# A second pair of bf16 q/k buffers, state transfers a chunk later, and a written order for the transfer queue, in a kernel of chunked mLSTM attention and a bilinear MLP

## Chip, cores and metric

One core of a Trainium2 chip runs the kernel. The metric is device time in microseconds; several runs are taken, and their median counts. Five engines work side by side: PE (matmul), DVE (vector), ACT (scalar), POOL (GpSimd) and SP, which here does nothing but issue DMA transfers.

## The reference

The first part is an mLSTM recurrence over 768 tokens for 4 batches of 8 heads of width 40; the second is a bilinear MLP on the 3072 tokens of 320 channels.

```python
for t in range(S):
    m_new = np.maximum(f_gate[:, :, t] + m, i_gate[:, :, t])
    f_stab = np.exp(f_gate[:, :, t] + m - m_new)
    i_stab = np.exp(i_gate[:, :, t] - m_new)
    C = f_stab * C + i_stab * einsum('bhd,bhe->bhde', vt, kt)
    n = f_stab * n + i_stab * kt
    denom = np.maximum(np.abs(n . qt), 1.0)
    y[:, :, t] = sigmoid(o_gate[:, :, t]) * (C qt) / denom
x = y.transpose(0, 2, 1, 3).reshape(B * S, H * D)
out = ((x @ w_a) * (x @ w_b)) @ w_out
```

(The indices that broadcast are left out.) All inputs and the output are float32.

## The kernel before

**Chunks and blocks.** The recurrence is computed chunk by chunk: 24 chunks `n`, six spans of 128 tokens for each of four batches, numbered so that a batch comes again after four chunks. A chunk needs its own q, k, v and gates and the state that the same batch's last chunk left. The MLP works on nine blocks of two or three chunks (`sizes`). `run_block(kb)` puts the MLP of block `kb` and the attention of block `kb + 1` into one order on PE: after each MLP matmul it gives out as many steps of `attention()` as are due by a count (`units`), so that attention is done shortly before its block's MLP ends. From block 2 on, PE's order is exactly this written one; the other queues are ordered by a scheduler, by when it thinks things come due.

**A late chunk** (n from 6 on) is a set of generators, each a stage cut at its `yield`s, and the string `PATTERN` says whose next step comes. `stage_a(n+1)` splits q and k into three bf16 pieces: ACT casts the first (L432), DVE makes the others, all in a `qks` buffer, one for q and one for k, and SP transposes it to `T` (L446, two transfers a buffer; `T` too has one buffer for q and one for k). `stage_b` computes the scores `pS` from `T` (L469), weighs them by the gate table `E` (a tile `gbc`, L474) and casts them to `pb` (L476, L480). `stage_i` computes `pI` from q and the state `cx` (L495). `stage_c` computes `pV` from `pb`, `E` and v (L521), so it is the last reader of that `gbc` tile; there are two `gbc` buffers, and `load_g` (L180) fills one for chunk n + 2. `stage_u` updates the state `cst` (`pU`, L545), splits it into `cb`, sends that to `c_dram` and reads it back as `cx`, side by side as PE needs it (L573 to L577). `stage_e(n+1)` masks the gate table on POOL (L407) and takes its exponentials on ACT (L414). `stage_f` divides by the denominator and multiplies by the output gates `osig` (L597, L600, L602); `load_o` loads four chunks' gates at once and ACT takes their sigmoid (L167). `stage_d` transposes the result to `xh`, `xl` for the MLP (L620 to L626).

**The MLP of a block** runs over 12 groups `ff` of 128 hidden units. `up` makes two products `pu_ff_0` and `pu_ff_1` of eight matmuls each (L729; three PSUM buffers for all `pu`); ACT (DVE for two groups) copies the first to `g` (L736), DVE multiplies it with the second (L737) and splits it into `gh` and `gl` (L739, L741). `down`, two groups later, adds into `pd` (L702). After the last group ACT copies each `pd` to a tile `o` (L711) and SP stores it (L712). The tiles `g` and `o` have one tag, `acp`, with three buffers.

**The gates** of all chunks are computed once at the start, in scratch tiles `gfim`, `g_tab` and `g_b`; the conversion of the MLP's weights uses the two `qks` buffers as its scratch (`step`) before attention needs them.

Of the kernel before, what the change touches and what calls it, by code (L numbers as in the profile page):

```python
# [8 lines left out]
F32 = mybir.dt.float32  # L9
BF16 = mybir.dt.bfloat16  # L10
# [10 lines left out]
def kernel(  # L21
# [45 lines left out]
    for x in qk:  # L67
        nc.gpsimd.memset(x[..., D:], 0.0)
    va = [wpool.tile([P, H, DV], F32, name=f"va{j}") for j in range(NQ)]
    qks2 = [wpool.tile([P, 2, H, P], BF16, name=f"qks{j}") for j in range(2)]  # L70

    step = [
        x.rearrange("p w h t -> p (w h t)").bitcast(F32)[:, j * WCH:(j + 1) * WCH]
        for j in range(2) for x in qks2
    ]
    HH = H // 2

# [74 lines left out]
    def load(n):  # L152
        with tc.issue_after(issued.get(("v", n - 1), issued["w"])):
            load_qk(n)
            load_v(n)
# [28 lines left out]

        return x.bitcast(BF16).rearrange("p h (d w) -> p h d w", w=2)[:, :, :, 1]

    gfim = wpool.tile([3 * BH, S], F32, name="gfim")
    gf, gi, gm = (gfim[j * BH:(j + 1) * BH] for j in range(3))
    tab = wpool.tile([3 * BH, NC, P], F32, name="g_tab")
    gbt = wpool.tile([3 * BH, 2, P], F32, name="g_b")  # L190
    gb3 = [gbt[j * BH:(j + 1) * BH] for j in range(3)]

    def fetch_gates(cols):
        for t, x in ((gf, f_gate), (gi, i_gate)):
# [223 lines left out]
    def stage_a(n):  # L418

        c, b = chunks[n]  # L420
        s = st.setdefault(n, {})
        src = nat(n)[0][..., 0:D]
        need(32)
        for _ in conv:
            pass

        at = {"h": (0, 2 * D), "m": (D, D), "l": (2 * D, 0)}
        s["T"] = []
        for j in range(2):
            qks = qks2[j]  # L430
            ph, pm, pl = (qks[:, 1, :, at[i][j]:at[i][j] + D] for i in "hml")
            nc.scalar.copy(ph, src[:, j])  # L432
            yield
            r = apool.tile([P, H * DV], F32, tag="tmp", name=f"r{n}_{j}")[:, 0:H * D]
            r = r.rearrange("t (h d) -> t h d", h=H)
            (nc.gpsimd if 2 * n + j < 4 else nc.vector).tensor_tensor(r, src[:, j], ph, op=ALU.subtract)  # L436
            nc.vector.tensor_copy(pm, r)
            yield
            (nc.gpsimd if n < 8 else nc.vector).tensor_tensor(pl, r, pm, op=ALU.subtract)
            yield  # L440
            lo = (1 - j) * D
            nc.vector.tensor_copy(qks[:, 0, :, lo:lo + 2 * D], qks[:, 1, :, D - lo:3 * D - lo])
            nc.vector.tensor_copy(qks[:, 0, :, 2 * D * j:2 * D * j + D], ph)  # L443
            T = apool.tile([P, 2, H, P], BF16, tag=f"T{j}", name=f"T{n}_{j}", bufs=1)
            for w in range(2):
                nc.sync.dma_start_transpose(T[:, w], qks[:, w].rearrange("t h d -> t (h d)"))  # L446
            s["T"].append(T)
            yield
# [84 lines left out]
    def stage_u(n):  # L533
        c, b = chunks[n]
        if c == NC - 1:
            return
        s = st[n]
        if n < 6:
            pU = ps_dn.tile([P, 512], F32, tag="pd2", name=f"pU{n}")
        else:  # L540
            pU = ps_at.tile([P, 512], F32, tag="pat", name=f"pU{n}")
        pu = pU[:, 0:HH * DV].rearrange("p (h d) -> p h d", h=HH)
        for h in range(H):
            r, _, x = half(h)
            nc.tensor.matmul(  # L545
                pu[r:r + 64, x], nat(n)[0][:, 1, h, :], s["vw"][:, h], start=True, stop=True
            )
# [12 lines left out]
        cb = apool.tile([P, 3, HH, DV], BF16, tag="cb", name=f"cb{n}", bufs=1)  # L560
        cr = apool.tile([P, H * DV], F32, tag="tmp", name=f"cr{n}")[:, 0:HH * DV]
        cr = cr.rearrange("t (h d) -> t h d", h=HH)
        nc.scalar.copy(cb[:, 2], t)
        nc.gpsimd.tensor_tensor(cr, t, cb[:, 2], op=ALU.subtract)
        yield
        if n < 8:
            nc.scalar.copy(cb[:, 1], cr)
        else:
            nc.vector.tensor_copy(cb[:, 1], cr)
        nc.gpsimd.tensor_tensor(cb[:, 0], cr, cb[:, 1], op=ALU.subtract)  # L570
        for j in range(2):
            cd = c_dram[b][:, :, j * HH:(j + 1) * HH].rearrange("i d h e -> d i h e")
            nc.sync.dma_start(cd[:, 3], cb[j * 64:j * 64 + D, 2])  # L573
            nc.sync.dma_start(cd[:, 0:3], cb[j * 64:j * 64 + D])
        for w in range(2):
            nc.sync.dma_start(
                cx[b][w], c_dram[b][w:w + 3].rearrange("i d h e -> (i d) h e")  # L577
            )
        yield

    def stage_f(n):
        s = st[n]
        num = s["num"]
        nq = num[:, :, D]
        den = apool.tile([P, H], F32, tag="den", name=f"den{n}")
        if chunks[n][0] == 0:
            nc.vector.tensor_scalar(den, nq, -1.0, 1.0, op0=ALU.mult, op1=ALU.max)
            nc.vector.scalar_tensor_tensor(den, nq, 1.0, den, op0=ALU.mult, op1=ALU.max)
        else:
            nc.vector.scalar_tensor_tensor(den, nq, -1.0, nq, op0=ALU.mult, op1=ALU.max)  # L590
            nc.vector.tensor_scalar_max(den, den, 1.0)
        after["r", n] = nc.vector.reciprocal(den, den).ins  # L592
        yield
        c, b = chunks[n]
        y = osig[c][:, b]
        yv = y[:, 0:DM].rearrange("p (h d) -> p h d", h=H)
        (nc.vector if n < NS else nc.gpsimd).tensor_tensor(  # L597
            yv, yv, den.unsqueeze(2).broadcast_to([P, H, D]), op=ALU.mult
        )
        nc.vector.tensor_tensor(yv, num[:, :, 0:D], yv, op=ALU.mult)  # L600

        nc.scalar.copy(y[:, DM:], y[:, 2 * P:DM])  # L602
        s["y"] = y
        yield

# [23 lines left out]
        yield ("done", n)  # L629


    PATTERN = "bebebBeBeBeiaaadadadoaaavcvcfufuu"

    def ahead(n):
        if n + 1 < NCH:
            if n > NS:
                with tc.issue_after(issued["w"]):
                    load(n + 1)
        if NE <= n + 2 < NCH:
            load_g(n + 2)  # L640

    def gates_in(n):
        if n % B == 0 and n > 0:
            load_o(n // B)

    def early_chunk(n):
        yield from begin_b(n)
        yield from begin_i(n)
        if n > NS:
            yield from stage_d(n - 1)  # L650
        gates_in(n)
        yield from (begin_e if n + 1 < NE else stage_e)(n + 1)
        if n + 1 < NF32:
            yield from begin_a(n + 1)
        else:
            yield from stage_a(n + 1)
            yield from stage_v(n + 1)
        yield from begin_c(n)
        yield from stage_u(n)
        yield from stage_f(n)  # L660

    def late_chunk(n):
        more = n + 1 < NCH
# [314 lines left out]
    def rest():  # L978
# [75 lines left out]
```

## Time and profile before

| | us |
|---|---|
| runs: median (lowest to highest) | 583.01 (582.88 to 584.32) |
| the profiled execution | 583.91 |
| its span, first to last instruction | 582.1 |
| PE busy | 545.8 (94%) |
| DVE busy | 411.3 (71%) |
| ACT busy | 225.6 (39%) |
| POOL busy | 126.2 (22%) |

The profile shows one execution. Busy times overlap, and matmuls are pipelined, so 94% is no measure of PE's pace: that is told by the granted clock, 0.950 in the mean of the span. Views of the trace name an instruction by engine, line and tiles, and give the idle time of its engine just before it with what ended it; "SPq" is SP's issuing of transfers.

### The profile page before, as it was taken

What the parts mean: (1) busy time and instruction counts of PE and PEld (TensorE: products, weight loads), DVE (VectorE), ACT (ScalarE), POOL (GpSimd) and SP (SyncE); (2) the same over time, 40 slices, a digit from 0 to 9 for tenths busy, and PEclk for the clock granted to TensorE, in tenths of its full rate; (3) what the DMA queues carried; (4) which work ended last, traced back from release to release, by engine and by line L of the source; (5) the groups of instructions that cost most, each with busy time, mean ns of one, the idle gap of its engine ahead of it and who ended that gap; (6) DMA issues with size and microseconds to landing.
All of it is one profiled execution on the core that took longest, in us unless ns stands there. A gap on an engine that the chain in (4) does not pass through costs nothing.

```text
span 582.1 us, 12451 instructions
## 1 busy us (share of the span) xinstructions
PE 545.8 (94%) x4810; PEld 515.7 (89%) x4810; DVE 411.3 (71%) x949; ACT 225.6 (39%) x548; POOL 126.2 (22%) x181
## 2 busy tenths in 40 slices
PE   9687899998999997999799998999989999999997
PEld 6585799988998996999799997998989999999997
DVE  6899776469978883887749876778848675944332
ACT  5677745334432542332523432523313533311111
POOL 2011235253331230332221340331211202000000
PEclk9686679998999997999899999999989999999999
DMA  9999513577949745478555577486536532400000
GB/s 177 288 269 270 116 32 90 114 105 159 157 115 149 147 92 106 84 150 162 103 125 101 116 124 134 112 158 141 92 85 122 113 73 90 56 1 24 0 1 35
DMA packets 198679, 66.77 MB, mean 115 GB/s; under 512 B 184252, under 2 KB 191900, under 8 KB 198620
## 3 DMA queue, kind: packets, MB, share of 16 engines
q1 hardware_dynamic: 198620, 65.98, 55.1%
q8 instruction: 38, 0.62, 0.5%
q14 instruction: 21, 0.17, 0.1%
HBM read 41.11 MB, written 5.97 MB: 81 GB/s over the span
## 4 chain that ended last, share of the span: by engine, by line
PE 71%; issue 6%; DMA 4%; DVE 3%; SPq 2%; ACT 1%; POOL 1%; POOLq 0%; ACTq 0%; DVEq 0%
PE pu L729 40%; PE pd L702 18%; DMA T<-qks 4%; PE pV L521 3%; PE pS L469 2%; PE pU L545 2%; SPq L446 1%; PE pS L803 1%; PE pV L855 1%; PE pX L620 1%; PE pI L495 1%; PE pI L824 1%; DVE g L737 1%; PE pT L790 0%; POOL osig L597 0%
## 5 line engine op out<-in xcount | busy, mean ns | idle before, releaser
L729 PE MATMUL pu<-xh,w 128*128 128x384 f32 (+1 forms) x1080 | 289.5, 333 | 4.2 <-ACT g L736 1.8
L729 PE MATMUL pu<-xl,w 128*128 128x384 f32 (+1 forms) x648 | 211.8, 329 | 1.0 <-DVE xl L626 1.0
L729 PEld LDWEIGHTS pu<-xh,w 128*128 128x128 f32 x1080 | 196.6, 196 | 7.9 <-DVE w L374 3.0
L702 PE MATMUL pd<-w,gh 128*128 128x320 f32 x576 | 133.8, 319 | 8.8 <-DVE gh L739 8.0
L729 PEld LDWEIGHTS pu<-xl,w 128*128 128x128 f32 x648 | 126.9, 196 | 1.6 <-DVE xl L626 1.3
L702 PEld LDWEIGHTS pd<-w,gh 128*128 128x128 f32 x576 | 99.6, 194 | 10.2 <-DVE gh L739 8.9
L737 DVE TENSOR_TENSOR g<-pu,g 128x384 f32<-128x384 f32 (+1 forms) x108 | 54.7, 506 | 52.2 <-PE pu L729 49.0
L702 PE MATMUL pd<-w,gl 128*128 128x320 f32 x288 | 91.1, 322 | 0.1
L736 ACT COPY g<-pu 128x384 f32<-128x384 f32 (+1 forms) x92 | 40.4, 439 | 76.8 <-PE pu L729 69.5
L456 POOL TENSOR_TENSOR vr<-va 128x336 f32<-128x336 f32 x18 | 14.5, 804 | 203.0 <-PE pV L521 203.0
L702 PEld LDWEIGHTS pd<-w,gl 128*128 128x128 f32 x288 | 54.9, 193 | 0.9 <-DVE gl L741 0.6
L432 ACT CAST qks<-qk 128x320 bf16<-128x320 f32 x36 | 16.5, 458 | 96.2 <-DMA T<-qks 84.5
L414 ACT ACTIVATE gbc<-gbc,gtab 128x128 f32<-128x128 f32 x160 | 49.3, 389 | 9.9 <-POOL gbc L407 9.8
L741 DVE TENSOR_TENSOR gl<-g,gh 128x384 fp32r<-128x384 f32 (+1 forms) x92 | 48.3, 525 | 1.3
L443 DVE COPY qks<-qks 128x320 bf16<-128x320 bf16 x36 | 10.6, 296 | 42.4 <-ACT qks L432 37.6
L739 DVE CAST gh<-g 128x384 fp32r<-128x384 f32 (+1 forms) x96 | 36.4, 379 | 1.4
L476 ACT CAST pb<-gbc 128x512 bf16<-128x512 f32 x36 | 22.1, 613 | 27.3 <-DVE gbc L474 27.3
L436 DVE TENSOR_TENSOR r<-qk,qks 128x320 f32<-128x320 f32 x36 | 26.1, 725 | 2.1 <-ACT qks L432 2.1
L597 POOL TENSOR_TENSOR osig<-osig,den 128x320 f32<-128x320 f32 x22 | 15.9, 723 | 53.5 <-DVE den L592 43.6
L407 POOL TENSOR_SCALAR_AFFINE_SELECT gbc<-gbc 128x1024 f32<-128x1024 f32 x20 | 24.4, 1221 | 14.1 <-DMA gbc<-g_dram 13.5
L521 PEld LDWEIGHTS <-pb 128*128 128x128 bf16 x576 | 23.1, 96 | 4.0 <-DVE pb L480 1.6
L469 PE MATMUL pS<-T,T 120*128 120x128 bf16 x288 | 23.3, 223 | 3.4 <-DMA T<-qks 2.9
(129 smaller groups left out, 801.0 us busy)
## 6 DMA issues: line engine op xcount, KB each, us to landing
gbc<-g_dram SPq DMA_DIRECT2D x20, 512.0 KB
qk<-in_q_dram SPq DMA_DIRECT2D x24, 160.0 KB
qk<-in_k_dram SPq DMA_DIRECT2D x24, 160.0 KB
va<-in_v_dram SPq DMA_DIRECT2D x24, 160.0 KB
osig<-in_o_gate_dram SPq DMA_DIRECT2D x24, 160.0 KB
raw<-in_moe_w_out_dram SPq DMA_DIRECT2D x12, 320.0 KB
out_dram<-o SPq DMA_DIRECT2D x24, 160.0 KB
raw<-in_moe_w_a_dram SPq DMA_DIRECT2D x8, 384.0 KB
```

What stands on the lines that cost most here:

```text
L407: nc.gpsimd.affine_select(E, E, pattern=[[0, H], [1, P]], compare_op=ALU.is_ge, fill=-1e30, base=0, channel_multiplier=-1,)
L414: nc.scalar.activation(E[:, h], E[:, h], AF.Exp, bias=beta[:, h:h + 1])
L436: (nc.gpsimd if 2 * n + j < 4 else nc.vector).tensor_tensor(r, src[:, j], ph, op=ALU.subtract)
L469: nc.tensor.matmul(pS[:, x, :], kT[0:K3, w, h, :], qT[0:K3, w, h, :], start=(w == 0), stop=(w == 1))
L476: nc.scalar.copy(pb[:, 0], E)
L521: nc.tensor.matmul(pv[:, h], pb[i][:, h % HH, :], vb[j][:, h], start=(x == 0), stop=(x == len(terms) - 1),)
L702: nc.tensor.matmul(pd[t][:, 0:DM], a[:, cols], w, start=(ff == 0 and first), stop=(ff == NF - 1 and last),)
L729: up_in = nc.tensor.matmul(acc[j], a, r, start=(x == 0), stop=(x == len(terms) - 1),).ins
L736: (nc.vector.tensor_copy if kb > 0 and ff in [1, 2] else nc.scalar.copy)(g, acc[0])
L737: nc.vector.tensor_tensor(g, acc[1], g, op=ALU.mult)
L739: (nc.vector.tensor_copy if kb > 0 else nc.scalar.copy)(gh, g)
L741: (nc.gpsimd if kb * 12 + ff < 16 else nc.vector).tensor_tensor(gl, g, gh.bitcast(F32), op=ALU.subtract)
```

## The change

There are four `qks` buffers, two pairs, used by even and odd chunks in turn. The second pair's memory is that in which the gates' scratch lies at the start of the program: `ga` holds the gates and `g_b`, `gt` the table. `stage_u` leaves its split state in `states`; the writing to `c_dram` and the reading back to `cx` are calls that the next chunk makes. The loads of q, k, v, of the gate table, of the output gates and these two calls are letters of the new `PATTERN` ("L", "G", "O", "P", "C"), which `aside` serves; q, k and v are now loaded two chunks ahead, where it was one. The 64-column copy at the end of `stage_f` goes from ACT to DVE from chunk 6 on. From block 2 on SP, too, issues in the order in which the code is written.

```diff
-    qks2 = [wpool.tile([P, 2, H, P], BF16, name=f"qks{j}") for j in range(2)]
+    qks2 = [wpool.tile([P, 2, H, P], BF16, name=f"qks{j}") for j in range(4)]
...
-        for j in range(2) for x in qks2
+        for j in range(2) for x in qks2[0:2]
...
-    gfim = wpool.tile([3 * BH, S], F32, name="gfim")
-    gf, gi, gm = (gfim[j * BH:(j + 1) * BH] for j in range(3))
-    tab = wpool.tile([3 * BH, NC, P], F32, name="g_tab")
-    gbt = wpool.tile([3 * BH, 2, P], F32, name="g_b")
-    gb3 = [gbt[j * BH:(j + 1) * BH] for j in range(3)]
+    ga, gt = (x.rearrange("p w h t -> p (w h t)").bitcast(F32)[0:3 * BH] for x in qks2[2:4])
+    gf, gi, gm = (ga[j * BH:(j + 1) * BH, 0:S] for j in range(3))
+    gb3 = [ga[j * BH:(j + 1) * BH, S:].rearrange("p (w t) -> p w t", w=2) for j in range(3)]
+    tab = gt[:, 0:S].rearrange("p (c t) -> p c t", c=NC)
...
-            qks = qks2[j]
+            qks = qks2[2 * (n % 2) + j]
...
-        for j in range(2):
-            cd = c_dram[b][:, :, j * HH:(j + 1) * HH].rearrange("i d h e -> d i h e")
-            nc.sync.dma_start(cd[:, 3], cb[j * 64:j * 64 + D, 2])
-            nc.sync.dma_start(cd[:, 0:3], cb[j * 64:j * 64 + D])
-        for w in range(2):
-            nc.sync.dma_start(
-                cx[b][w], c_dram[b][w:w + 3].rearrange("i d h e -> (i d) h e")
-            )
-        yield
+        states[n] = cb
+        yield
+    def put_state(n):
+        if n in states:
+            b = chunks[n][1]
+            for j in range(2):
...
+                nc.sync.dma_start(cd[:, 0:3], states[n][j * 64:j * 64 + D])
+    def get_state(n):
+        if states.pop(n, None) is not None:
...
+                    cx[b][w], c_dram[b][w:w + 3].rearrange("i d h e -> (i d) h e")
...
-        nc.scalar.copy(y[:, DM:], y[:, 2 * P:DM])
+        (nc.scalar.copy if n < NF32 else nc.vector.tensor_copy)(y[:, DM:], y[:, 2 * P:DM])
...
-    PATTERN = "bebebBeBeBeiaaadadadoaaavcvcfufuu"
-    def ahead(n):
-        if n + 1 < NCH:
-            if n > NS:
-                with tc.issue_after(issued["w"]):
-                    load(n + 1)
-        if NE <= n + 2 < NCH:
+    PATTERN = "LbababPaBaBaBaiaaGvdvdCedOeeececfufuu"
+    STEPS = sum(o.islower() or o == "B" for o in PATTERN)
+    def aside(o, n):
+        if o == "L" and n + 2 < NCH and n + 2 > NS + 1:
+            with tc.issue_after(issued["w"]):
+                load(n + 2)
+        if o == "P":
+            put_state(n - 1)
+        if o == "G" and NE < n + 2 < NCH:
             load_g(n + 2)
-    def gates_in(n):
-        if n % B == 0 and n > 0:
+        if o == "C":
+            get_state(n - 1)
+        if o == "O" and n % B == 0 and n > 0:
             load_o(n // B)
...
-        units = (36 if kb < 2 else len(PATTERN)) * sizes[kb + 1] if kb + 1 < NB else 1
+        units = (36 if kb < 2 else STEPS) * sizes[kb + 1] if kb + 1 < NB else 1
...
-    with tc.manual_schedule(engines={mybir.EngineType.PE}):
+    with tc.manual_schedule(engines={mybir.EngineType.PE, mybir.EngineType.SP}):
```

Lines of the changed program lie a few numbers off: the transposes are L445 there, the out stores L726, the `g` copy L750, the `cx` loads L587. The number at the end of a tile's name tells its instances apart.

On SP, where block 2 ends and block 3 begins, the order before is this (`o_0` to `o_2` are block 2's output tiles, `gbc_2922` the gate table of a later chunk):

```order
L446 DMA_TRANSPOSE T_1_3148<-qks_90 128x8x128
L446 DMA_TRANSPOSE T_0_3048<-qks_89 128x8x128 x2
L446 DMA_TRANSPOSE T_1_3148<-qks_90 128x8x128
L712 DMA out_dram<-o_0_3120 128x320
L712 DMA out_dram<-o_1_3123 128x320
L712 DMA out_dram<-o_2_3126 128x320
L180 DMA gbc_2922<-g_dram 128x1024
L148 DMA va_87<-in_v_dram 128x8x40
```

and after the change, at the same place on SP:

```order
L445 DMA_TRANSPOSE T_0_2988<-qks_91 128x8x128 x2
L445 DMA_TRANSPOSE T_1_3045<-qks_92 128x8x128 x2
L180 DMA gbc_3056<-g_dram 128x1024
L587 DMA cx_0_99<-c_dram_124 120x336
L587 DMA cx_1_100<-c_dram_124 120x336
L726 DMA out_dram<-o_0_3131 128x320
L726 DMA out_dram<-o_1_3134 128x320
L726 DMA out_dram<-o_2_3137 128x320
L142 DMA qk_81<-in_q_dram 128x8x40
```

The gate load and two state loads have moved ahead of the three stores. `gbc_3056` takes the buffer that `pV` of the current chunk reads last, and that `pV` stands on PE behind twelve `pu` matmuls of block 3. The same holds at the four boundaries that follow (at the last of them, 6 to 7, without `cx`).

On ACT, at the same boundary, the order before is:

```order
L711 COPY o_0_3120<-pd_0_2176 128x320
L711 COPY o_1_3123<-pd_1_2177 128x320
L711 COPY o_2_3126<-pd_2_2178 128x320
L736 COPY g_0_3151<-pu_0_0_3132 128x384
L563 CAST cb_3258<-cst_93 128x168
```

and after the change:

```order
L725 COPY o_0_3131<-pd_0_2187 128x320
L725 COPY o_1_3134<-pd_1_2188 128x320
L725 COPY o_2_3137<-pd_2_2189 128x320
L562 CAST cb_3262<-cst_95 128x168
L750 COPY g_0_3157<-pu_0_0_3143 128x384
L413 ACTIVATE gbc_3056<-gbc_3056,gtab 128x128 x8
```

ACT's rows have hardly moved. `g_0` takes the buffer of `o_0`, so its copy waits for `o_0`'s store, before as after.

On SP, in the last chunks, the order before is:

```order
L446 DMA_TRANSPOSE T_1_6753<-qks_90 128x8x128 x2
L446 DMA_TRANSPOSE T_0_6634<-qks_89 128x8x128 x2
L712 DMA out_dram<-o_0_6726 128x320
L712 DMA out_dram<-o_1_6729 128x320
L712 DMA out_dram<-o_2_6732 128x320
L180 DMA gbc_6476<-g_dram 128x1024
L446 DMA_TRANSPOSE T_1_7005<-qks_90 128x8x128 x2
L446 DMA_TRANSPOSE T_0_6972<-qks_89 128x8x128 x2
```

and after the change:

```order
L445 DMA_TRANSPOSE T_0_6551<-qks_89 128x8x128 x2
L445 DMA_TRANSPOSE T_1_6628<-qks_90 128x8x128 x2
L180 DMA gbc_6635<-g_dram 128x1024
L726 DMA out_dram<-o_0_6737 128x320
L726 DMA out_dram<-o_1_6740 128x320
L726 DMA out_dram<-o_2_6743 128x320
L445 DMA_TRANSPOSE T_0_6902<-qks_91 128x8x128 x2
L445 DMA_TRANSPOSE T_1_6962<-qks_92 128x8x128 x2
```

The q pair (`T_0`) now stands ahead of the k pair (`T_1`), and the pairs of neighbouring chunks read different `qks` buffers.

More of the change, by code (lines that the diff above doesn't have):

```diff
@@ L570, in stage_u @@
         nc.gpsimd.tensor_tensor(cb[:, 0], cr, cb[:, 1], op=ALU.subtract)
-        for j in range(2):
-            cd = c_dram[b][:, :, j * HH:(j + 1) * HH].rearrange("i d h e -> d i h e")
-            nc.sync.dma_start(cd[:, 3], cb[j * 64:j * 64 + D, 2])
-            nc.sync.dma_start(cd[:, 0:3], cb[j * 64:j * 64 + D])
-        for w in range(2):
-            nc.sync.dma_start(
-                cx[b][w], c_dram[b][w:w + 3].rearrange("i d h e -> (i d) h e")
-            )
-        yield
+        states[n] = cb
+        yield
+    states = {}
+    def put_state(n):
+        if n in states:
+            b = chunks[n][1]
+            for j in range(2):
+                cd = c_dram[b][:, :, j * HH:(j + 1) * HH].rearrange("i d h e -> d i h e")
+                nc.sync.dma_start(cd[:, 3], states[n][j * 64:j * 64 + D, 2])
+                nc.sync.dma_start(cd[:, 0:3], states[n][j * 64:j * 64 + D])
+    def get_state(n):
+        if states.pop(n, None) is not None:
+            b = chunks[n][1]
+            for w in range(2):
+                nc.sync.dma_start(
+                    cx[b][w], c_dram[b][w:w + 3].rearrange("i d h e -> (i d) h e")
+                )
     def stage_f(n):
@@ L629, in stage_d @@
         yield ("done", n)
-    PATTERN = "bebebBeBeBeiaaadadadoaaavcvcfufuu"
-    def ahead(n):
-        if n + 1 < NCH:
-            if n > NS:
-                with tc.issue_after(issued["w"]):
-                    load(n + 1)
-        if NE <= n + 2 < NCH:
+    PATTERN = "LbababPaBaBaBaiaaGvdvdCedOeeececfufuu"
[7 more added lines that the diff above has]
+        if o == "G" and NE < n + 2 < NCH:
             load_g(n + 2)
-    def gates_in(n):
-        if n % B == 0 and n > 0:
+        if o == "C":
+            get_state(n - 1)
+        if o == "O" and n % B == 0 and n > 0:
             load_o(n // B)
     def early_chunk(n):
+        aside("L", n)
         yield from begin_b(n)
         yield from begin_i(n)
+        aside("P", n)
         if n > NS:
             yield from stage_d(n - 1)
-        gates_in(n)
+        aside("O", n)
         yield from (begin_e if n + 1 < NE else stage_e)(n + 1)
+        aside("C", n)
+        aside("G", n)
         if n + 1 < NF32:
@@ L662, in late_chunk @@
     def late_chunk(n):
-        more = n + 1 < NCH
         parts = {
@@ L667, in late_chunk @@
         }
-        if more:
+        if n + 1 < NCH:
             parts |= {"e": stage_e(n + 1), "a": stage_a(n + 1), "v": stage_v(n + 1)}
         for o in PATTERN:
-            if o == "o":
-                gates_in(n)
-            elif o in parts:
+            if o in parts:
                 x = next(parts[o], "end")
@@ L676, in late_chunk @@
                     yield x
+            else:
+                aside(o, n)
         for g in parts.values():
@@ L681, in attention @@
         for n in range(NS, NCH):
-            ahead(n)
             yield from (early_chunk if n < NF32 else late_chunk)(n)
@@ L993, in rest @@
             squash(0, b, 1)
-        for n in range(max(NS, NE), NS + 2):
-            with tc.issue_after(issued["w"]):
-                load_g(n)
+        load_g(NE)
         yield from attention()
```

## The prediction

> **What bounds the kernel now.** I read the summary of the chain that ended last first, then the waits, then the stretches around PE's idle times.
>
> ```profile
> PE 71%; issue 6%; DMA 4%; DVE 3%; SPq 2%; ACT 1%; POOL 1%; POOLq 0%; ACTq 0%; DVEq 0%
> PE pu L729 40%; PE pd L702 18%; DMA T<-qks 4%; PE pV L521 3%; PE pS L469 2%; PE pU L545 2%; SPq L446 1%; PE pS L803 1%; PE pV L855 1%; PE pX L620 1%; PE pI L495 1%; PE pI L824 1%; DVE g L737 1%; PE pT L790 0%; POOL osig L597 0%
> ```
>
> The chain is PE for 71%, nearly all of it MoE matmuls, whose number the change leaves alone. What a reordering can win is PE's idle time and the clock lost after it. The only transfer with weight in the chain is the transpose `T<-qks`. The waits (total us, times, longest) name who stands behind it:
>
> ```profile
> ACT qks L432 <- DMA T<-qks: 84.5, 26, 7.7
> PE pd L702 <- DVE gh L739: 8.0, 3, 4.0
> ACT g L736 <- DMA out_dram<-o: 3.3, 3, 1.1
> ```
>
> ACT waits 84.5 us to overwrite a `qks` buffer that the transposes still read. Most of this costs nothing, since PE holds work. Where it costs, the timeline shows (start, us, engine, line, idle before):
>
> ```profile
> 217.01 6.25 SPq L446 DMA_TRANSPOSE T<-qks  x4
> ...
> 224.06 0.46 ACT L432 CAST qks<-qk 128x320 bf16<-128x320 f32 x1 [7.72 <-DMA T<-qks]
> ...
> 224.42 0.47 ACT L736 COPY g<-pu 128x384 f32<-128x384 f32 x1
> ...
> 225.82 0.55 DVE L737 TENSOR_TENSOR g<-pu,g 128x384 f32<-128x384 f32 x1
> ...
> 226.82 0.90 PE L702 MATMUL pd<-w,gh 128*128 128x320 f32 x2 [4.04 <-DVE gh L739]
> ```
>
> SP's four transposes issue until 223.26; ACT's cast waits for them; the gate copy `g` stands behind the cast; its product and cast on DVE follow; PE idles 4.04 us. Three more idle times have the same head, a late ACT queue or the DVE copies behind it, and one pair sits together at 282 to 286:
>
> ```profile
> 282.63 0.56 PE L495 MATMUL pI<-cx,T 120*128 120x42 bf16 x16 [1.50 <-DVE gbc L474]
> ...
> 285.93 0.44 PE L729 MATMUL pu<-xh,w 128*128 128x384 f32 x1 [1.76 <-ACT g L736]
> ...
> 360.16 0.56 PE L702 MATMUL pd<-w,gh 128*128 128x320 f32 x2 [2.20 <-DVE gh L739]
> ...
> 425.49 0.56 PE L702 MATMUL pd<-w,gh 128*128 128x320 f32 x2 [1.73 <-DVE gh L739]
> ```
>
> **What goes.** With two pairs of `qks`, chunk n+1 is cast while the transposes of chunk n still read theirs, so ACT's cast does not wait for them and `g` is not late. These idle times sum to 4.04 + 1.50 + 1.76 + 2.20 + 1.73 = 11.2 us. The clock behind them is in the table by stretches; its columns are the stretch, its length, busy us (instructions) of PE, PEld, DVE, ACT and POOL, then the granted clock, the DMA share and GB/s:
>
> ```profile
> 220.00:240.00 20.00, 15.96 (x138) 14.99 (x138) 8.30 (x20) 3.63 (x9) 4.15 (x5) 0.83 0.55 110
> 280.00:300.00 20.00, 16.73 (x111) 15.94 (x110) 13.46 (x30) 9.40 (x22) 1.86 (x3) 0.91 0.41 91
> 350.00:370.00 20.00, 17.76 (x159) 16.43 (x157) 11.27 (x29) 6.58 (x12) 1.92 (x3) 1.00 0.66 140
> 420.00:440.00 20.00, 18.24 (x153) 17.16 (x152) 10.00 (x26) 4.05 (x11) 4.02 (x5) 0.91 0.58 110
> ```
>
> Three of the four places lost clock: 0.17 · 20 + 2 · 0.09 · 20 = 7.0 us, of which some 0.7 lies in the idle times themselves; so 6.3. The saving is **17.5 us**. A wider bound from below is 0 (the casts are late for another reason). The pair at 282 to 286 is the least sure, since ACT's gate sigmoid stood before it.
>
> A page of the Trainium skill says when clock is lost: "TensorE: Matmul & The Clock Gate", section "Part 1: The HAM clock gate (the "warmup" mystery)", puts the drop to half speed behind an idle window of about 3.4 us. By that only the 4.04 us stall would have cost clock, and of the new ones below only the longest: about -14.1 + 11.7 + 1.8 + 1.5 + 2.0 = +2.9, against the +3.1 that I reach, the same side. This trace differs from the rule: the stretch with the 1.73 us stall shows 0.91, and the one with 2.20 us shows 1.00.
>
> **What is new: the block's start.** The out stores of a block now stand on SP behind the gate load of chunk n+2, and that load waits for `pV` of chunk n, which PE does only inside the new block. The tile `o_0` shares a buffer with the new block's `g_0`, so ACT's copy of `g_0` waits for the out store to land. Before, the stores left at once:
>
> ```profile
> 297.17 1.34 SPq L712 DMA_DIRECT2D out_dram<-o  x3
> ...
> 299.12 0.48 ACT L736 COPY g<-pu 128x384 f32<-128x384 f32 x1 [1.09 <-DMA out_dram<-o]
> ...
> 301.25 0.33 SPq L180 DMA_DIRECT2D gbc<-g_dram  x1
> ```
>
> The first store needs 1.95 us from issue to the copy. PE's stretch there, from the chain:
>
> ```profile
> 297.56 2.46 PE pu L729 x14
> 300.02 1.22 PE pV L521 x48
> 301.24 1.86 PE pu L729 x10
> 303.10 0.60 PE pU L545 x16
> 303.70 2.11 PE pu L729 x11
> ```
>
> A matmul takes 2.46 / 14 = 0.176 us. In the changed order `pV` stands behind 12 of them, so it ends at 12 · 0.176 + 1.22 = 3.3 us after the block's start S. Then SP issues `gbc` (0.42 to the next issue) and two `cx` loads:
>
> ```profile
> 286.00 0.78 SPq L576 DMA_DIRECT2D cx<-c_dram  x2
> ```
>
> With 0.1 between them, the store leaves at S + 4.6 and lands at S + 6.55 by the row above. If it queues behind `gbc`, the price is bounded by that load's own landing:
>
> ```profile
> 459.01 0.34 SPq L180 DMA_DIRECT2D gbc<-g_dram  x1
> ...
> 462.66 1.09 POOL L407 TENSOR_SCALAR_AFFINE_SELECT gbc<-gbc 128x1024 f32<-128x1024 f32 x1 [0.99 <-DMA gbc<-g_dram]
> ```
>
> 3.65 us behind S + 3.3, and about 1 us (an estimate: half of the 1.95) for the store: S + 8.0. The copy adds 0.48. `pu` has three buffers, so the fourth group, `pu_1_1`, needs that copy; it is due after 24 matmuls, `pV` and `pU`, at S + 303.70 - 297.56 = S + 6.1. The stall is 0.9 to 2.4 us; I take 2.0, nearer to the load's row, since SP issues the load first. This holds at blocks 2 to 3, 3 to 4 and 4 to 5. At 5 to 6 `pV` stands behind 17 matmuls (S + 4.2) and `pU` behind `pu_1_1` (due at S + 5.4): 2.5 to 3.9, taken 3.5. At 6 to 7 the tiles are narrower:
>
> ```profile
> 485.52 1.43 PE pu L729 x12
> 486.95 1.24 PE pV L521 x48
> ```
>
> 0.12 us a matmul; `pV` behind 10 ends at S + 2.4, `pu_1_1` is due at S + 4.6. There `g_0` also stands behind a score cast `pb`, which is ready at about S + 5.7: 1.4 to 2.9, taken 2.2. In sum 6.0 + 3.5 + 2.2 = **11.7 us** (6.5 to 14.0).
>
> The Trainium skill, "DMA: Bandwidth & Descriptors", section "Queues, rings and completion order", has descriptors of one ring consumed in order on each DMA engine; that rule speaks against this change: by it the sum is 14.0 in place of 11.7, and the whole +5.4 in place of +3.1. No run here shows a store behind a `gbc` load.
>
> Of the clock: three of four such stalls lost some 2.1 us each; I take three of these five at 1.8, **5.4 us** (0 to 9).
>
> **What is later elsewhere.** The output gates' load now stands behind the `gbc` load, so ACT's sigmoid comes later:
>
> ```profile
> 270.53 2.73 SPq L160 DMA_DIRECT2D osig<-in_o_gate_dram  x4
> ...
> 276.21 1.28 ACT L167 ACT_TABLE_LOAD   x1 [2.94 <-DMA osig<-in_o_gate_dram]
> ```
>
> It takes 5.7 us from issue to landing; at three chunks ACT then holds the second `pb` behind it. Bounded by nothing and one such landing less the chunk's slack, 0 to 4: I take **1.5**. In the last chunk:
>
> ```profile
> 492.13 6.38 SPq L446 DMA_TRANSPOSE T<-qks  x4
> ...
> 493.72 0.57 PE L495 MATMUL pI<-cx,T 120*128 120x42 bf16 x16
> ...
> 501.15 0.62 PE L469 MATMUL pS<-T,T 120*128 120x128 bf16 x8
> ```
>
> Before, the k pair went out first at 492.13. Now the q pair goes first, and it needs the buffer that `pI` reads until 494.3, with the k pair queued behind. All four end 2.2 us later (494.3 against 492.13). If they landed just in time for 501.15 before, PE waits 2.2; if earlier, less; I take **2.0** (0 to 3.3). In ordinary chunks, of three tiles a block, more MoE work stands between `pI` and the next scores, and the same 2.2 us stay covered.
>
> **What costs nothing.** Of ACT's 24 copies of 64 columns, 18 go to DVE:
>
> ```profile
> L602 ACT COPY osig<-osig x24: 244/245/247, 17.3 to 511.0; 128x64 f32<-128x64 f32 x24
> ```
>
> 18 · 0.25 = 4.5 us on DVE spread over 18 chunks, beside PE's MoE work; without that cover it would be the same 4.5 us on PE's path. The states' write and read a chunk later unblock SP's queue, and `cx` is first needed three chunks after. The four added memsets, the gates' tables inside `qks` and the earlier q, k, v loads are covered by the same MoE work. I take 0 for all of these, nothing and 4.5 being the bounds.
>
> **Sum**, against the profiled execution of 583.91: -17.5 + 11.7 + 5.4 + 1.5 + 2.0 = +3.1, 587.0. The runs' median, 583.01, lies 0.9 below that execution, so I give **586.1**.
>
> **Rivals.** (1) Faster: the removed stalls go, and the new ones of about 2 us leave the clock alone, as the 2.20 us one at 360 did. Then -17.5 + 11.7 + 1.5 + 2.0 = -2.3, so 580.7. It decides once the new stalls lose less than 2.3 us of clock in all. If the stores also overtake the `gbc` load (6.5) and the two small terms are nothing, it is -11.0, so 572.0. For it speaks the stall at 360; against it, that the one of 1.73 us and the pair lost clock. (2) The terms cancel: within 1.75 us of 583.0, say with the clock's loss at 1. (3) Slower on one mechanism alone: SP's order makes the out store wait, from the point where it lands over 5.6 us after S (6.1 less the copy); at the upper end of 14.0, clock 9.0 and the saving without the pair at 282 (17.5 - 3.3 - 1.8 = 12.4), +14.1: 597.1. It shares its sign with the forecast and is its tail. (4) The change does not do what it says: the casts no longer wait, but `T` still has one buffer a side, so the transposes themselves start no earlier, and `g` is late behind something else. Saving half, 8.7, gives +11.9, 594.9.
>
> **Chances.** Forecast 0.41, (1) 0.34, (2) 0.15, (3) and (4) together 0.10. A measurement of this kernel tells about 0.3%, 1.75 us, from no change. Faster by more 0.34, within 0.15, slower by more 0.51. The range leaves a tenth out on each side: from 574.0, inside (1), to 595.0. The forecast's own range, beside a likely faster case, is 584.8 (583.01 and 0.3%) to 591 (the stalls at 14.0 and 2.6 more of clock).
>
> **What would show it.** Right: ACT's wait for `T<-qks` before the casts gone; PE's idle times at the blocks' ends gone; instead, at five block starts, `out_dram<-o` issued behind `gbc<-g_dram`, the copy of `g` waiting for that store, and PE idle 1 to 4 us before `pu`, with the clock under 1.0 behind it. Wrong: stores that land within 5.6 us of the block's start; no such idle time; a clock of 1.00 behind it; or `T<-qks` still the releaser of a wait that PE feels. `pS` in the last chunks waiting for `T`, and `pX` waiting for the gates, would show the smaller terms.

## The result, and the profile after

The changed kernel takes 590.34 us (median of 4 runs, 589.26 to 591.32) against 583.66 (582.88 to 584.85; one run more than in the table above) for the kernel before, a ratio of 1.0112 with the 95% interval 1.0085 to 1.0139: **slower by some 1%**, which is clear of the noise. The profiled execution took 591.32 us, with a span of 589.5 against 582.1, so the profiles have +7.4 us to explain.

The summary of the chain that ended last, after the change, by engine and by line:

```profile
PE 69%; DMA 7%; DVE 4%; ACT 3%; issue 3%; SPq 2%; POOL 1%; POOLq 0%; ACTq 0%; DVEq 0%
PE pu L743 39%; PE pd L716 18%; PE pV L520 3%; DMA out_dram<-o 3%; PE pS L468 2%; PE pU L544 1%; DMA osig<-in_o_gate_dram 1%; PE pX L630 1%; SPq L587 1%; PE pI L494 1%; PE pS L817 1%; DMA T<-qks 1%; PE pV L869 1%; ACT gbc L413 1%; SPq L160 1%
```

`DMA T<-qks` has fallen from 4% of the span to 1%, and `DMA out_dram<-o`, which had no entry, holds 3%. The waits (total us, times, longest us):

```profile
PE pu L743 <- ACT g L750: 17.5, 7, 4.5
ACT g L750 <- DMA out_dram<-o: 15.3, 5, 9.0
...
ACT qks L431 <- DMA T<-qks: 8.7, 3, 4.9
```

The casts' wait for the transposes went from 84.5 to 8.7 us; the `g` copy's wait for the out store from 3.3 to 15.3. PE's own timeline has the five idle times of the forecast nowhere, and five others instead, one at the start of each of blocks 3 to 7:

```profile
235.26 0.69 PE L743 MATMUL pu<-xh,w 128*128 128x384 f32 x1 [2.88 <-ACT g L750]
...
302.30 0.45 PE L743 MATMUL pu<-xh,w 128*128 128x384 f32 x1 [2.44 <-ACT g L750]
...
368.13 0.67 PE L743 MATMUL pu<-xh,w 128*128 128x384 f32 x1 [2.58 <-ACT g L750]
...
435.00 0.69 PE L743 MATMUL pu<-xh,w 128*128 128x384 f32 x1 [4.51 <-ACT g L750]
...
496.10 0.38 PE L743 MATMUL pu<-xh,w 128*128 128x256 f32 x1 [3.03 <-ACT g L750]
```

They sum to 15.4 us. The chain in order of time (start, us, what) shows how one of them comes about, at the start of block 4:

```profile
293.52 2.11 PE pu L743 x12
295.63 1.24 PE pV L520 x48
296.88 0.34 SPq L180
...
298.19 3.48 DMA out_dram<-o
...
301.77 0.49 ACT g L750
302.26 0.04 issue
302.30 2.73 PE pu L743 x10
```

Twelve `pu` matmuls, then `pV`, then the gate load that waited for it, then (behind two `cx` loads) the store, then the copy of `g_0`, and only then PE's fourth `pu` group. Read it from the bottom: each piece starts when the one above ends.

Of the clock, the stretches that hold a stall (columns as in the prediction; the granted clock is the third number from the end):

```profile
220.00:240.00 20.00, 17.12 (x152) 16.16 (x151) 11.14 (x28) 5.68 (x17) 5.04 (x7) 0.91 0.64 123
...
300.00:320.00 20.00, 17.70 (x160) 17.04 (x161) 17.01 (x39) 7.78 (x18) 2.72 (x4) 0.91 0.58 114
...
360.00:380.00 20.00, 17.42 (x168) 16.15 (x167) 13.60 (x36) 8.09 (x17) 5.15 (x7) 0.91 0.62 124
...
420.00:440.00 20.00, 15.49 (x133) 14.49 (x132) 7.50 (x21) 4.91 (x15) 3.28 (x4) 0.83 0.38 94
...
480.00:500.00 20.00, 16.97 (x169) 16.56 (x167) 10.61 (x27) 6.68 (x16) 3.29 (x4) 1.00 0.27 68
```

Four of the five stalls lost clock: 3 · 0.09 · 20 + 0.17 · 20 = 8.8 us.

At the end of block 2, where ACT's copy of `g` stood behind a late cast before, it now has no cast ahead of it and waits only for PE:

```profile
220.74 0.48 ACT L750 COPY g<-pu 128x384 f32<-128x384 f32 x1 [1.37 <-PE pu L743]
```

### The profile page after: what moved, and what is told of

Read it like the earlier page. It is cut to its first block, busy times and chain, and to the rows that moved or that the text cites. A ratio compares the mean times of both kernels' runs of the same rounds, so it can differ in the third digit from the quotient of the medians.

```text
span 589.5 us, 12444 instructions
## 1 busy us (share of the span) xinstructions
PE 546.1 (93%) x4810; PEld 516.2 (88%) x4810; DVE 408.6 (69%) x967; ACT 221.8 (38%) x530; POOL 125.0 (21%) x185
## 4 chain that ended last, share of the span: by engine, by line
PE 69%; DMA 7%; DVE 4%; ACT 3%; issue 3%; SPq 2%; POOL 1%; POOLq 0%; ACTq 0%; DVEq 0%
PE pu L743 39%; PE pd L716 18%; PE pV L520 3%; DMA out_dram<-o 3%; PE pS L468 2%; PE pU L544 1%; DMA osig<-in_o_gate_dram 1%; PE pX L630 1%; SPq L587 1%; PE pI L494 1%; PE pS L817 1%; DMA T<-qks 1%; PE pV L869 1%; ACT gbc L413 1%; SPq L160 1%
## 5 line engine op out<-in xcount | busy, mean ns | idle before, releaser
L743 PEld LDWEIGHTS pu<-xh,w 128*128 128x128 f32 x1080 | 198.6, 197 | 25.2 <-ACT g L750 19.4
L743 PE MATMUL pu<-xl,w 128*128 128x384 f32 (+1 forms) x648 | 214.2, 333 | 1.0 <-DVE xl L636 1.0
L716 PEld LDWEIGHTS pd<-w,gh 128*128 128x128 f32 x576 | 98.4, 191 | 1.7 <-ACT gh L753 1.2
L750 ACT COPY g<-pu 128x384 f32<-128x384 f32 (+1 forms) x92 | 40.5, 441 | 139.6 <-PE pu L743 116.5
L716 PE MATMUL pd<-w,gl 128*128 128x320 f32 x288 | 89.9, 318 | 0.0
L755 DVE TENSOR_TENSOR gl<-g,gh 128x384 fp32r<-128x384 f32 (+1 forms) x92 | 50.3, 548 | 1.6
L527 DVE TENSOR_TENSOR num<-pV,num 128x336 f32<-128x336 f32 x18 | 9.1, 506 | 38.9 <-PE pV L520 38.8
L753 DVE CAST gh<-g 128x384 fp32r<-128x384 f32 (+1 forms) x96 | 34.0, 355 | 1.6
L562 ACT CAST cb<-cst 128x168 bf16<-128x168 f32 x18 | 6.0, 332 | 62.4 <-DMA gbc<-g_dram 40.8
L473 DVE TENSOR_TENSOR gbc<-pS,gbc 128x512 f32<-128x512 f32 x36 | 24.6, 683 | 5.2 <-PE pS L468 5.1
L520 PE MATMUL pV<-va,pb 128*128 128x42 bf16 x288 | 25.1, 182 | 1.6 <-DVE pb L479 1.6
```

The costliest lines, as they stand in the source:

```text
L473: nc.vector.tensor_tensor(E, pS, E, op=ALU.mult)
L520: nc.tensor.matmul(pv[:, h], pb[i][:, h % HH, :], vb[j][:, h], start=(x == 0), stop=(x == len(terms) - 1),)
L716: nc.tensor.matmul(pd[t][:, 0:DM], a[:, cols], w, start=(ff == 0 and first), stop=(ff == NF - 1 and last),)
L743: up_in = nc.tensor.matmul(acc[j], a, r, start=(x == 0), stop=(x == len(terms) - 1),).ins
L750: (nc.vector.tensor_copy if kb > 0 and ff in [1, 2] else nc.scalar.copy)(g, acc[0])
L753: (nc.vector.tensor_copy if kb > 0 else nc.scalar.copy)(gh, g)
```

## The experiments

Times are medians; each ratio is against the kernel before on the same chip, and its medians there were 583.10 (e runs), 583.04 (f) and 581.99 us (g and h). The first four ask whether the store's wait is the loss, and whether the second pair is the gain.

**e1: the gate load behind the stores.**

```diff
-    PATTERN = "LbababPaBaBaBaiaaGvdvdCedOeeececfufuu"
+    PATTERN = "LbababPaBaBaBaiaavdvdCedGOeeececfufuu"
```

> The changed kernel with the letter G (gate load of chunk n + 2) two letters later in PATTERN, so that SP issues a block's out stores ahead of the gate load that waits for pV; nothing else differs. Theory A (the stores wait behind that load, g_0 waits for its buffer): the five idle times of 2.88, 2.44, 2.58, 4.51 and 3.03 us before pu go (15.4 us), and the clock lost behind four of them (0.09 x 20 x 3 + 0.17 x 20 = 8.8 us, some 1 of it inside the idle times) with them: about 23 below the changed kernel's 590, so 567. Rival B (g_0 is late at the block's start because ACT is, its state cast or its exponentials standing ahead, and the store only lands last): the idle times stay, 588 to 591. Rival C (the stalls go, but their time was slack that returns as waits for a later gate table): 575 to 585.

Measured 566.75 us, ratio 0.9721 (0.9677 to 0.9765). All five idle times are gone, and PE's idle times of over 0.4 us after 100 us sum to 9.7 us, against 24.2 in the changed kernel and 17.7 before. Theory A holds, and so does the size: 567 was expected.

**e2: the out tiles in the buffers of `gl`.**

```diff
-                    o = mpool.tile([P, NTB], F32, tag="acp", name=f"o{kb}_{t}")[:, 0:DM]
+                    o = mpool.tile([P, NTB], F32, tag="gl", name=f"o{kb}_{t}")[:, 0:DM]
```

> The changed kernel with its output tiles in the buffers of gl instead of those of g, SP's order untouched: the stores leave as late as now, but g_0 no longer needs a buffer that they read. Theory A: the wait of ACT's g copy for the store goes, and with it most of the five idle times; gl_0 on DVE then waits for the store instead, with more slack, so 0 to 1 us a block may stay: 567 to 572. Rival B (ACT itself is late): 588 to 591. Rival D (the gate load's traffic slows what PE needs, whatever the buffers): 580 to 590.

Measured 568.13 us, 0.9745 (0.9716 to 0.9773). SP's issues around the start of block 3 (start, us, what):

```profile
226.07 0.35 SPq L180 DMA_DIRECT2D gbc<-g_dram  x1
226.53 0.82 SPq L587 DMA_DIRECT2D cx<-c_dram  x2
227.40 1.41 SPq L726 DMA_DIRECT2D out_dram<-o  x3
```

and ACT's copy of `g` there:

```profile
224.18 0.48 ACT L750 COPY g<-pu 128x384 f32<-128x384 f32 x1 [0.99 <-PE pu L743]
```

The stores leave behind the load as in the changed kernel, yet `g_0` is copied 3.2 us before the first of them is issued. So two links are both needed: the stores' place behind the waiting load, and the buffer that `o_0` and `g_0` share. Either one broken gives back 22 to 24 us.

**e3: the second pair alone, in the kernel before.**

```diff
-    qks2 = [wpool.tile([P, 2, H, P], BF16, name=f"qks{j}") for j in range(2)]
+    qks2 = [wpool.tile([P, 2, H, P], BF16, name=f"qks{j}") for j in range(4)]
...
-            qks = qks2[j]
+            qks = qks2[2 * (n % 2) + j]
```

(The gates' scratch lies in the second pair, as in the change.)

> The kernel before with the second pair of qks buffers (and the gates' scratch inside it) and nothing else of the change. Theory A: the five idle times of before (4.04, 1.50, 1.76, 2.20, 1.73; 11.2 us) and 6.3 us of clock go: 566. Rival E (the saving needs the new order of letters too, since T still has one buffer a side and the scheduler's SP order stays): the casts' wait for T goes, but half or less of the idle time: 575 to 583.

Measured 579.73 us (575.07 to 582.73), 0.9938 (0.991 to 0.9966). A gain of some 3 us, not 17: the time of rival E, but not its reason, since the casts still wait 70.0 us for the transposes. ACT at the end of block 2:

```profile
221.50 0.46 ACT L431 CAST qks<-qk 128x320 bf16<-128x320 f32 x1 [6.34 <-DMA T<-qks]
221.87 0.47 ACT L735 COPY g<-pu 128x384 f32<-128x384 f32 x1
```

The cast ahead of `g` still waits for transposes. With four buffers the scheduler lets ACT cast a chunk further ahead: in ACT's order the row ahead of `g_11` of block 2 is now `qks2_91<-qk1_81`, the q of chunk 13, and its buffer is the one from which SP is transposing chunk 11. The wait has moved with the freedom.

**e4: the changed kernel with one pair.**

```diff
-            qks = qks2[2 * (n % 2) + j]
+            qks = qks2[j]
```

> The changed kernel with stage_a using one pair of qks buffers for all chunks, as before; order of letters, states a chunk later and SP's written order stay. Theory A: the five stalls at the blocks' starts stay and the casts' wait for T returns with idle times at the blocks' ends: 600 to 608. Rival E (what removed the old idle times was the new order, not the buffers): within 3 us of 590.

Measured 590.51 us (585.1 to 593.64), 1.0117 (1.0055 to 1.0178): the same as the changed kernel. The casts wait 67.1 us for the transposes again, and none of the old idle times returns. The second pair is not needed to remove them, and by e3 it is not enough.

The next four take e1 and undo one part each, to find what did.

**f1: e1 with one pair** (the edit of e4).

> The kernel of e1_gate_behind_stores with one pair of qks buffers for all chunks. With one pair ACT's cast of the next q stands ahead of g_11 again, as in the kernel before, and waits for the transposes. Theory P (what removed the old idle times at the blocks' ends is that SP sends the transposes earlier, with no state transfer ahead of them): 565 to 570, as with two pairs. Theory Q (the second pair carries a good part of it once the stores are out of the way): 573 or more.

**f2: e1 with the states at once.**

```diff
         states[n] = cb
+        put_state(n)
+        get_state(n)
         yield
```

> The kernel of e1_gate_behind_stores with the states written and read back at the end of their own chunk, so that SP waits for cb on POOL and for the round trip through c_dram ahead of the next transposes. Theory P: the transposes of a block's last chunk are late again; what ACT casts ahead of g_11 reads the other pair, so the idle time shows as pS or pI waiting for T instead, or as a late q load: 572 to 582. Theory Q (two pairs are enough): 565 to 570.

**f3: e1 with SP's order left to the scheduler.**

```diff
-    with tc.manual_schedule(engines={mybir.EngineType.PE, mybir.EngineType.SP}):
+    with tc.manual_schedule(engines={mybir.EngineType.PE}):
```

> The kernel of e1_gate_behind_stores with SP's order left to the scheduler, as before the change. There ACT casts the chunk after next ahead of g_11 (it reads the pair that SP is transposing), and SP's transposes stand in k, q order around the cx loads. Theory R (the written order of SP, through the loads of q and k, is what keeps the casts away from the block's end): the idle times at the blocks' ends return, 572 to 580. Theory P (the states a chunk later are enough): 565 to 570.

**f5: e1 with the old letters.**

```diff
-    PATTERN = "LbababPaBaBaBaiaavdvdCedGOeeececfufuu"
+    PATTERN = "LPbebebBeBeBeiaaadadCadOaaavcGvcfufuu"
```

> The kernel of e1_gate_behind_stores with the letters of the old PATTERN (a after i, e between b, the gate load behind pV), the new calls for loads and states placed among them, SP's written order kept. Theory P: no cast stands ahead of g_11 and no state transfer ahead of the transposes, so 565 to 572. Theory S (the new letters, which start the casts a third of a chunk earlier, carry the saving): 575 to 585.

| e1 with | us | ratio (95%) |
|---|---|---|
| nothing undone | 566.75 | 0.9721 (0.9677 to 0.9765) |
| f1: one pair | 568.67 | 0.9749 (0.9715 to 0.9784) |
| f2: states at once | 568.81 | 0.977 (0.9724 to 0.9816) |
| f5: old letters | 568.83 | 0.9749 (0.9727 to 0.9771) |
| f3: SP scheduled | 575.95 | 0.9852 (0.9807 to 0.9898) |

Pair, states and letters can each be taken back with no loss that these runs can tell: each median is some 2 us above e1's, but the intervals overlap. f2 goes against theory P's reason: SP issues the `cx` loads ahead of the block's last transposes there, and nothing is lost. The loads of q, k and v two chunks ahead and the copy moved to DVE were not taken back alone. SP's written order cannot go: without it the idle times before `pd` at the blocks' ends return, as here in f3:

```profile
226.73 0.56 PE L716 MATMUL pd<-w,gh 128*128 128x320 f32 x2 [1.51 <-DVE gh L753]
```

e1 and f3 both have two pairs and differ in SP's order alone. In e1, as in the changed kernel, no cast stands ahead of block 2's last `g`; in f3 ACT casts q of the chunk after next there, and the cast waits. The written order has that q loaded only behind the block's end (SP issues the load at 229.78 us in e1, at 206.61 in f3), so that in e1 the cast cannot come so early; this is theory R. With one pair the cast stands ahead of `g` under the written order too, and yet does no harm; why, f1 and f3 show side by side. SP at the end of block 2 in f1:

```profile
214.71 6.16 SPq L445 DMA_TRANSPOSE T<-qks  x4
220.98 0.98 SPq L587 DMA_DIRECT2D cx<-c_dram  x2
```

SP there in f3:

```profile
215.21 2.63 SPq L445 DMA_TRANSPOSE T<-qks  x2
217.95 0.52 SPq L587 DMA_DIRECT2D cx<-c_dram  x1
218.56 2.61 SPq L445 DMA_TRANSPOSE T<-qks  x2
```

ACT's cast of a later q, which stands ahead of `g_11` (block 2's last `g`), in f1:

```profile
220.83 0.46 ACT L431 CAST qks<-qk 128x320 bf16<-128x320 f32 x1 [3.44 <-DMA T<-qks]
221.19 0.47 ACT L750 COPY g<-pu 128x384 f32<-128x384 f32 x1
```

and in f3:

```profile
224.85 0.46 ACT L431 CAST qks<-qk 128x320 bf16<-128x320 f32 x1 [4.99 <-DMA T<-qks]
225.22 0.47 ACT L750 COPY g<-pu 128x384 f32<-128x384 f32 x1
```

The four begin within 0.5 us of each other. In f1 the q pair goes first; in f3 the k pair and a `cx` load do, and q follows 3.85 us later than in f1. The cast that needs q's buffer starts 4.0 us later. f1 and f3 differ in the pairs too; g5 tests the place of the q pair alone.

**g5: f1 with the k pair first.**

```diff
-            for w in range(2):
-                nc.sync.dma_start_transpose(T[:, w], qks[:, w].rearrange("t h d -> t (h d)"))
             s["T"].append(T)
+            for i in (1, 0) if j == 1 else ():
+                for w in range(2):
+                    nc.sync.dma_start_transpose(s["T"][i][:, w], qks2[i][:, w].rearrange("t h d -> t (h d)"))
```

> The kernel of f1_stores_first_one_pair with a chunk's four transposes issued together, k pair first, q pair last; the casts and everything else are in the order that this leaves. Theory T (the q cast ahead of g_11 waits for the q pair, so its place among the transposes decides): idle times of 1 to 3 us before pd at the blocks' ends return, 573 to 582. Theory P (what counts is when the four begin): 566 to 571.

Measured 578.61 us, 0.9938 (0.9914 to 0.9961), 10 above f1 (which ran on another chip). Idle times before `pd` at the blocks' ends are back:

```profile
227.92 0.42 PE L717 MATMUL pd<-w,gh 128*128 128x320 f32 x1 [1.02 <-DVE gh L754]
...
358.11 0.57 PE L717 MATMUL pd<-w,gh 128*128 128x320 f32 x2 [1.32 <-DVE gh L754]
...
423.85 0.56 PE L717 MATMUL pd<-w,gh 128*128 128x320 f32 x2 [0.62 <-DVE gh L754]
```

They are 3.0 of the 10 us; other waits (before `pX` and in the first late chunks) and the clock, 0.953 against 0.961, make the rest. Theory T holds for the place, and only for part of the time. The edit also delays the issue of the q pair until k is ready, so it is harsher than a mere exchange.

**g1: the written queue alone, in the kernel before.**

```diff
-    PATTERN = "bebebBeBeBeiaaadadadoaaavcvcfufuu"
+    PATTERN = "bebebBeBeBeiaaadadadoaaavcGvcfufuu"
...
-    with tc.manual_schedule(engines={mybir.EngineType.PE}):
+    with tc.manual_schedule(engines={mybir.EngineType.PE, mybir.EngineType.SP}):
```

(In `late_chunk`, G calls `load_g(n + 2)`, and `ahead` does so only for earlier chunks.)

> The kernel before with one part of the change: SP's order from block 2 on is the written one, and the gate load is moved from the chunk's head to behind pV (a written order with it at the head would stop the queue). One pair of qks, the old letters, states at once, the 64-column copy on ACT. Theory T (the saving is that the written order sends the q pair of transposes first and undivided, so that the cast standing ahead of g_11 is free earlier): 567 to 573. Theory P (the parts must come together): 576 to 583.

Measured 618.06 us, 1.0603 (1.055 to 1.0656): far outside both expectations. PE's wait for the transposes:

```profile
PE pS L469 <- DMA T<-qks: 39.3, 25, 5.9
```

It was 2.9 us in the kernel before. A written queue serves whatever stands first. Here q, k and v are loaded one chunk ahead, behind states that SP must wait for. The casts wait for these loads (11 times for q, 19.7 us), SP stops 16 times in front of its transposes until DVE's pieces are there (103.5 us), and everything behind it is late too. So the written order needs company: f1, f2 and f5 show that it can do without the pair, the states or the letters, one at a time, and g1 that it cannot do without all. Which of the other parts are enough was not tried.

**g4: a small load in the gate load's place.**

```diff
-    PATTERN = "LbababPaBaBaBaiaaGvdvdCedOeeececfufuu"
+    PATTERN = "LbababPaBaBaBaiaaGvdvdCedHOeeececfufuu"
...
+                nc.sync.dma_start(
+                    gbc[n + 2][:, 0:1, 0:8], g_dram[c:c + 1, b * H:b * H + 1, 0:8].broadcast_to([P, 1, 8])
+                )
+        if o == "H" and n >= NF32 and n + 2 < NCH:
+            c, b = chunks[n + 2]
+            nc.sync.dma_start(gbc[n + 2], g_dram[c:c + 1, b * H:(b + 1) * H, :].broadcast_to([P, H, P]))
```

> The changed kernel with the gate load cut in two from chunk 6 on: at its old place only 8 columns of one head (4 KB in all), which wait for the same pV, and the whole table behind the out stores. The stores are issued as late as in the changed kernel, but no 512 KB stand ahead of them in the queue. Theory F (a store behind the load lands only after it: 2.9 to 4.0 us from its issue to the g copy, against 1.95 without): the stall at the blocks' starts falls from 2.4 to 2.9 us to about 1 (0.9 by the predicted lower bound), 574 to 581 with the clock. Theory G (the late issue alone makes the stall): 588 to 591.

Measured 592.1 us, 1.0161 (1.0123 to 1.02). The five stalls themselves did as theory F says: 1.10, 1.44, 1.78, 3.25 and 1.21 us, 8.8 in place of 15.4. At the start of block 6, SP issues the first store in g4 here:

```profile
434.12 1.84 SPq L737 DMA_DIRECT2D out_dram<-o  x3
```

and ACT copies `g` here:

```profile
436.55 0.48 ACT L761 COPY g<-pu 128x384 f32<-128x384 f32 x1 [7.79 <-DMA out_dram<-o]
```

2.43 us, where the changed kernel has 430.50 to 434.47, 3.97 us. At the five places it is 2.0 to 2.6 us in g4 and 2.9 to 4.4 in the changed kernel, so the load's own 512 KB cost a store 0.9 to 1.8 us beside the late issue. The total did not fall, because the edit made new waits that theory F had not counted: before `pX` 0.6 to 1.65 us at six places, and 2.08 before `pu` at 220 us. All in all PE's idle times sum to 25.9 us, against 24.2 in the changed kernel. The time of g4 therefore says nothing for or against F; the stalls do.

**h1: e1 with the output gates ahead.**

```diff
-    PATTERN = "LbababPaBaBaBaiaavdvdCedGOeeececfufuu"
+    PATTERN = "LbababPaBaBaBaiaavdvdCedOGeeececfufuu"
```

> The kernel of e1_gate_behind_stores with the letter O ahead of G, so that the four output gate loads stand ahead of the gate load that waits for pV. The remaining idle times before pX (0.49, 1.05, 0.68, 0.99 us, each behind a late sigmoid) should go: 3 us, 562 to 566. If the gates are late for the buffer that pX reads and not for the queue, no change: 565 to 569.

Measured 564.27 us (562.6 to 565.01), 0.968 (0.9636 to 0.9724), the fastest of all, below both kernels compared here. Its interval overlaps e1's. Of e1's four waits before `pX` one of 0.50 is left (the one in the last chunk, 1.2 to 1.4, stands in all kernels), and the idle times sum to 6.8 us. Page of h1, busy times:

```profile
PE 537.9 (96%) x4810; PEld 510.1 (91%) x4810; DVE 409.3 (73%) x967; ACT 221.3 (39%) x530; POOL 125.5 (22%) x185
```

## Why the prediction was right, and where it was not

The forecast was +3.1 us, the medians moved by +6.7 (583.66 to 590.34), inside the range. The two terms of the new stalls were 7.1 us too small together (24.2 against 17.1); that the sum was off by only half of that is luck, since the other terms came out lower than forecast.

**The new stalls at the blocks' starts** were the right mechanism at the right five places, and e1 and e2 show it from two sides. The term was too small: 15.4 us for a forecast of 11.7, and over its upper end of 14.0. The step that was mis-sized is the store's landing. I took the stall nearer to the case of a store queued behind the load, but with only part of it; the traces have 4.02, 3.58, 2.92, 3.97 and 4.43 us from the first store's issue to the copy at the five boundaries (230.71 to 234.73 at the first) against 1.95 in the row that I used for the lower end. The gate load itself was slower, too: 3.9 to 4.5 us from its issue until POOL masks it, for 3.65 in my row, and the copy follows that mask within 0.45 to 0.97 us at all five. g4 shows that the load's data delays the store; whether the store stands behind these data in the queue or shares the DMA engines with them, these runs do not separate. The rule of the Trainium skill that I weighed ("DMA: Bandwidth & Descriptors", section "Queues, rings and completion order") had put the sum at 14.0, and was nearer than my choice.

**The clock behind them** cost 8.8 us for a forecast of 5.4: four of five stalls lost some, not three, and the longest lost twice as much. Which stalls lose is a matter of where they fall in time (last section), so that three of five was a guess.

**The saving** came in full at the five places: 11.2 us of idle time are gone, and three small ones that I hadn't counted (0.61, 0.49 and 0.89) with them; and so are the four units of lost clock behind them (6.8 us for a forecast of 6.3). But the step that named its cause was wrong: "With two pairs of `qks` ... ACT's cast does not wait for them and `g` is not late". The changed kernel looks so, but the pair is neither enough nor needed. In e3, with two pairs, the casts wait 70.0 us and `g` is late; in e4 and f1, with one pair, the casts wait some 65 us, and `g` is on time all the same. What removed the idle times is SP's written order together with the other parts of the change: with two pairs it loads the next q too late for a cast to stand ahead of `g` (e1 against f3), and with one pair the q pair of transposes lands early enough (f1), which g5 shows for a part of the time only. The number was right for a reason that was not.

**The small terms.** Late output gates: 0.44 + 0.68 = 1.1 us before `pX` at 285 us (1.5 forecast). Last chunk: 0.80 before `pS` (2.0). Not forecast: 1.1 before `pu` at 215 us, where a cast and eight exponentials stand ahead of `g`, and 1.2 more between 120 and 146 us. In idle time the account closes: -11.2 - 2.0 + 15.4 + 1.1 + 0.8 + 1.1 + 1.2 = +6.4, as the two lists give (24.2 and 17.7). From 120 us on the clock was lost in six units of about 1.7 us (below), where it was five before; the span grew by 7.4, 0.7 less than idle time and clock together, in part since some of the slow clock falls on idle times.

**The rival "faster"**, by which stalls of about 2 us leave the clock alone, fell with the four rows at 0.91 and 0.83. The 2.20 us stall that spoke for it had lost nothing because of where it fell in time (last section).

## What to carry to other kernels

A queue in written order turns each entry that waits into a wait for all behind it: look what stands behind a load whose buffer is still read, and whose buffers those entries free. Here one letter's place was worth some 23 us, and one shared buffer tag nearly the same. And before crediting a saving to a part of a change, undo that part alone and try it alone: the second pair looked like the cause in every view, and was neither needed nor enough.

## What the runs showed of the hardware

The lost clock comes in units. In two-microsecond stretches behind the changed kernel's stall that ends at 302.30 the granted clock is:

```profile
302.00:304.00 2.00, 1.70 (x8) 1.70 (x9) 2.00 (x8) 1.97 (x4) 0.67 (x2) 0.83 1.33 182
304.00:306.00 2.00, 2.00 (x13) 1.70 (x12) 1.77 (x6) 2.00 (x8) 0.53 (x1) 0.50 0.51 74
306.00:308.00 2.00, 2.00 (x10) 2.00 (x10) 2.00 (x6) 1.29 (x4) 0.00 (x0) 0.81 0.08 20
```

(0.17 + 0.50 + 0.19) · 2 = 1.7 us lost, that is 3.4 us at half speed. The stall of 4.51 us lost twice that, 0.17 · 20 = 3.4 us; those of 2.44, 2.58 and 2.88 us one unit each; that of 3.03 us none, nor the one of 2.20 us in the kernel before, while one of 1.73 us did. The Trainium skill ("TensorE: Matmul & The Clock Gate", section "Part 1: The HAM clock gate (the "warmup" mystery)") has a window of about 3.4 us that runs freely. The unit agrees with that length; that a whole window must be idle does not, since 1.73 us were enough here.

The traces also show what decides beside the length. In each of the two kernels all slow stretches from 120 us on begin a multiple of 3.413 us apart: 122.42, 235.06, 303.33, 368.18 and 433.03 us in the changed kernel lie 33, 20, 19 and 19 of them from each other. Cut along this grid, the stall of 2.44 us lies in one window, and that of 3.03 us is split over two:

```profile
299.91:303.33 3.42, 1.03 (x6) 1.03 (x7) 3.42 (x7) 1.87 (x3) 2.29 (x3) 1.00 1.13 277
303.33:306.74 3.41, 3.41 (x17) 3.11 (x16) 3.18 (x9) 3.40 (x12) 0.53 (x1) 0.50 0.61 81
...
491.06:494.47 3.41, 2.01 (x21) 1.76 (x19) 2.41 (x8) 0.62 (x1) 1.98 (x3) 1.00 0.76 188
494.47:497.89 3.42, 1.79 (x16) 1.75 (x17) 2.27 (x6) 2.19 (x4) 1.09 (x1) 1.00 0.30 110
497.89:501.30 3.41, 3.41 (x45) 3.31 (x43) 2.94 (x9) 2.43 (x8) 0.00 (x0) 1.00 0.02 5
```

PE is idle for 2.39 us of the first window, and the next runs at half clock; it is idle for 1.40 and 1.63 us of the two others, and the clock stays. In the kernel before, the stall of 1.73 us lies in one window with 1.76 us of idle time and lost clock; that of 2.20 us is split into windows with 0.73 and 1.51 and lost none. Over all traces here, between 100 and 505 us, each window at full clock with 1.8 us or more of idle PE was followed by one at half clock, and of those with less than 1.75 only two were (0.40 and 1.37 us), so that idle time is not quite the whole of it. Where a stall falls on the grid is luck: the profiled execution of e4 has five such stalls (2.44, 2.59, 2.87, 4.58 and 2.87 us), but only two units lost behind them, and took 585.1 us, where the other three took 590.5 to 593.6.
